# Left-over values and the next chunk's left-over scores placed back to back in an attention loop

## The chip, the core and the metric

The kernel runs on one core of one Trainium2 chip. The metric is the device time of one execution in microseconds (us), measured over several executions; the profile is taken of one of them. In the profiles PE is TensorE (matmuls), PEld its weight loads, DVE the vector engine, ACT the scalar engine, and SP the engine that issues the DMAs (transfers). Ratios are the mean time of one kernel's runs over that of the other kernel's runs of the same rounds, so they are not quite the ratio of the medians quoted here.

Single executions of one kernel scatter by up to 2 us. I therefore use a second measure beside the time: in each trace, the distance from the start of the first column tile of the attention to the start of the last matmul of the kernel. It leaves out the start-up, the launch and the final stores. It is called "first tile to last matmul".

## The reference

It is a Conformer block on 2 x 4000 tokens of width 512: feed-forward, attention, convolution module, feed-forward. What matters here is the attention of one batch:

```python
q, k, v = h @ w_q, h @ w_k, h @ w_v                    # [2, 4000, 512]
scores = jnp.einsum('btd,bsd->bts', q, k) * scale
p = _softmax(scores, axis=-1)
attn = jnp.einsum('bts,bsd->btd', p, v) @ w_o
```

4000 keys are 31 tiles of 128 and 32 left over. That remainder is the subject of the change.

## The kernel before

Queries go in 16 chunks (8 for each batch) of 508 columns; the last chunk of each batch has 444. For each of 31 key tiles there are four score matmuls, an exponential on ACT, an addition to the sums on DVE, and, four tiles later, four value matmuls into four PSUM banks called Y.

```python
for kt in range(KT):                       # KT = 32; tile 31 is the left-over one
    if kt == self.TAIL_AT:                 # 18
        self.tail_scores(g)
    if kt < KT - 1:
        ...                                # 4 score matmuls, Exp, addition to acc
    if kt == KT - 1:
        self.split_sums(g)                 # ...
    def values(kt=kt, p=p, g=g, W=W):
        for dc in range(DC):
            ...                            # for kt == KT - 1: row tiles, K = 32
            self.mm(self.Yb[dc][:, 0:W], self.h[kt][r, dc * 128:(dc + 1) * 128], x[r, 0:W],
                    kt == 0, kt == KT - 1, ..., **at)
        if kt == KT - 1:
            self.finish_queries(g, done)   # copies the Y banks away, schedules projections
    self.lags.append(values)
    ...                                    # popped four tiles later
    hook(g, kt)                            # convolution projections of earlier chunks, loads
```

The left-over scores use a quarter of the array's columns each, so four of them run side by side as column tiles; each takes a quarter of the chunk's queries. The values use a quarter of the array's rows each, four of them side by side as row tiles. They need the same exponentials for all queries on each group of 32 partitions, so the result makes a trip through DRAM:

```python
def tail_scores(self, g):
    ...
    for cc in range(DC):                           # 16 matmuls, 128 rows x 32 columns
        for j, (r, q) in enumerate(parts):
            self.mm(ps[r, 0:n], hT[:, cc, r], self.qT[s][:, cc, q], ..., tile_position=(0, j * REST))
    self.act(self.pq[:, 0:n], ps[:, 0:n], AF.Exp, ...)
    for r, q in parts:
        ...                                        # 4 additions of 32 x 127 on DVE
    self.store(self.pqd[:, 0:n], self.pq[:, 0:n], ...)
    S.dma("SP", k, *[... e.dma_start(self.ptail[r, 0:W]...) for r, q in parts], ...)
```

After a chunk's queries are finished, the chunk goes through the output projection and a layer norm, whose result DMA transposes turn; the convolution projections of that chunk read it in the next chunk:

```python
if kt in (22, 27) and (0 <= g - 1 < tail or g - 1 == tail and (22, 27).index(kt) < self.KEEP):
    pair(g - 1, (22, 27).index(kt))                # two times four matmuls
```

## Time and profile before

| what | before |
|---|---|
| time, median of 4 | 2034.1 us (2033.78 to 2035.38) |
| span of the profiled run | 2030.5 us |
| TensorE busy | 2021.3 us, granted clock 0.999 |
| first tile to last matmul | 1540.93 us |
| visits to tiled mode (column or row tiles) | 32 |
| changes of tile shape | 64 |

The busy time says that TensorE's sequence sets the time, but it doesn't show the time lost between matmuls. What is lost when the tile shape changes is called a drain below. The prediction shows the lines and how the cost of a visit is read from starts.

### The profile page before, as it was taken

The numbers are of one execution on the slowest core, as the hardware profiler recorded it, in microseconds if no ns is written. First come the engines' busy times: TensorE is split into PE (matmuls) and PEld (weight loads), VectorE is DVE, ScalarE is ACT, GpSimd is POOL, SyncE is SP. The second block draws the span as 40 slices with busy tenths as digits, with TensorE's granted clock in tenths as the row PEclk, the third lists the DMA queues.
The fourth block names the chain that finished last, engine by engine and source line by source line (L and its number), as shares of the span: only waits on it lengthen the run. The fifth ranks groups of instructions, "written<-read, shape, count | busy, mean of one in ns | idle before, by whom it ended". The sixth has DMA issues, their size and how long they took to land.

```text
span 2030.5 us, 25096 instructions
## 1 busy us (share of the span) xinstructions
PE 2021.3 (100%) x9874; PEld 1026.5 (51%) x9874; DVE 1089.1 (54%) x2237; ACT 740.0 (36%) x1275; POOL 108.0 (5%) x235
## 2 busy tenths in 40 slices
PE   9999999999999999999999999999999999999998
PEld 5555555554444444445444444444455555555555
DVE  4234443335556667667766676667674543444433
ACT  3433333333333333333333333333345443443433
POOL 1000000000000000000000000000011000000000
PEclk9999999999999999999999999999999999999999
DMA  8122245421101111113521111111143111111111
GB/s 190 48 62 63 53 100 127 96 68 25 20 16 32 27 35 27 32 27 90 122 54 27 29 32 32 27 30 30 44 139 94 32 32 41 32 31 42 30 34 38
DMA packets 264644, 107.03 MB, mean 53 GB/s; under 512 B 204932, under 2 KB 264007, under 8 KB 264519
## 3 DMA queue, kind: packets, MB, share of 16 engines
q1 hardware_dynamic: 263841, 105.01, 21.7%
q8 instruction: 80, 1.31, 0.3%
q14 instruction: 45, 0.37, 0.1%
q10 hardware_dynamic: 678, 0.34, 0.1%
HBM read 35.81 MB, written 23.86 MB: 29 GB/s over the span
## 4 chain that ended last, share of the span: by engine, by line
PE 99%; DVE 0%; ACT 0%; DMA 0%; issue 0%; POOL 0%; DVEq 0%; ACTq 0%
PE s L521 56%; PE y L521 43%; DVE work L633 0%; DMA work<-work 0%; ACT work L571 0%; PE y L549 0%; POOL work L740 0%; PE y L536 0%; DVE work L1376 0%; DVE work L735 0%; DVE work L653 0%; DVE work L568 0%; DVE wff L1254 0%; ACT keys L571 0%; DVE wff L1141 0%
## 5 line engine op out<-in xcount | busy, mean ns | idle before, releaser
L571 ACT ACTIVATE work<-s 128x508 bf16<-128x508 f32 (+3 forms) x1044 | 613.8, 589 | 1197.8 <-PE s L521 1192.4
L521 PE MATMUL s<-work,wff 128*128 128x508 bf16 (+4 forms) x2640 | 628.3, 369 | 1.0 <-DMA work<-work 0.7
L521 PE MATMUL s<-work,keys 128*128 128x508 bf16 (+2 forms) x2240 | 505.8, 356 | 0.0
L521 PE MATMUL y<-wff,work 128*127 128x512 bf16 (+1 forms) x2000 | 501.4, 378 | 0.0
L521 PE MATMUL y<-work,keys 128*128 128x508 bf16 (+1 forms) x1984 | 495.1, 373 | 0.0
L971 DVE TENSOR_TENSOR work<-work 128x508 f32<-128x508 f32 (+1 forms) x480 | 324.3, 676 | 265.2 <-ACT work L571 262.5
L521 PEld LDWEIGHTS s<-work,wff 128*128 128x128 bf16 x2640 | 252.6, 98 | 277.1 <-issue 4.7
L521 PEld LDWEIGHTS y<-wff,work 128*127 128x127 bf16 x2000 | 274.4, 137 | 170.9
L521 PEld LDWEIGHTS s<-work,keys 128*128 128x128 bf16 (+1 forms) x2240 | 195.7, 97 | 228.9 <-ACT work L571 5.8
L521 PEld LDWEIGHTS y<-work,keys 128*128 128x128 bf16 x1984 | 192.1, 97 | 226.7 <-DVE work L568 0.5
L767 DVE SCALAR_TENSOR_TENSOR xt<-y,xt 127x512 bf16<-127x512 f32 x125 | 77.8, 684 | 364.2 <-PE y L521 364.2
L633 DVE BATCH_NORM_STATS2 work<-xt 127x6 f32<-127x512 bf16 x311 | 195.6, 679 | 4.7 <-DMA xt<-in_x_dram 4.6
L521 PE MATMUL s<-work 128*127 128x512 bf16 (+4 forms) x775 | 195.7, 377 | 1.2 <-DVE work L1372 1.2
L640 POOL TENSOR_TENSOR work<-work 127x4 f32<-127x4 f32 (+1 forms) x76 | 76.6, 1008 | 1127.8 <-DVE work L638 1127.8
L521 PEld LDWEIGHTS s<-work 128*127 128x127 bf16 (+2 forms) x775 | 94.3, 124 | 74.7 <-issue 3.0
L653 DVE TENSOR_SCALAR work<-xt,work 127x512 bf16<-127x512 bf16 x309 | 111.7, 408 | 27.6 <-POOL work L640 23.2
L767 DVE SCALAR_TENSOR_TENSOR xt<-s,xt 127x512 bf16<-127x512 f32 x55 | 38.1, 692 | 148.5 <-PE s L521 148.5
L571 ACT ACTIVATE wff<-s 128x508 f32<-128x508 f32 (+2 forms) x83 | 44.0, 531 | 64.2 <-PE s L521 64.1
L767 DVE SCALAR_TENSOR_TENSOR xt<-s,work,xt 127x512 bf16<-127x512 f32 x64 | 48.0, 750 | 31.0 <-PE s L521 30.5
L1152 DVE SCALAR_TENSOR_TENSOR wff<-wff,s 128x508 bf16<-128x508 f32 (+1 forms) x57 | 38.7, 679 | 42.0 <-PE s L521 41.9
L571 ACT ACTIVATE work<-keys,work 128x508 bf16<-128x508 bf16 (+1 forms) x68 | 52.2, 775 | 0.4 <-DVE work L1268 0.2
L1233 POOL COPY wff<-wff 128x1 bf16<-128x1 bf16 x56 | 10.5, 188 | 633.8 <-DVE wff L1152 631.0
(94 smaller groups left out, 439.9 us busy)
## 6 DMA issues: line engine op xcount, KB each, us to landing
keys<-keysd SPq DMA_DIRECT2D x62, 128.0 KB, 2.3
keysd<-work SPq DMA_DIRECT2D x14, 448.0 KB, 3.2
out_dram<-work SPq DMA_DIRECT2D x14, 448.0 KB, 3.2
dcvd<-wff SPq DMA_DIRECT2D x48, 127.0 KB, 1.8
keys<-dcvd SPq DMA_DIRECT2D x12, 508.0 KB, 4.8
xt<-in_x_dram SPq DMA_DIRECT2D x13, 448.0 KB, 4.7
wff<-in_w_ff_a_dram SPq DMA_DIRECT2D x15, 256.0 KB, 4.8
work<-work SPq DMA_TRANSPOSE x208, 2.5
```

The source lines that it names most:

```text
L521: self.S.op("PE", lambda e: e.matmul(out, lhsT, rhs, start=start, stop=stop, **kw), reads=reads, writes=[bank], inc=stop if inc is None el ...
L571: return self.S.op("ACT", lambda e: e.activation(out, in_, func, **kw), reads=reads, writes=writes)
L633: self.S.op("DVE", lambda e: e.bn_stats(self.st[sl][:, ti, 0:6], x), reads=[b_x], writes=[self.b_st[sl][ti]])
L640: S.op("POOL", lambda e: e.tensor_tensor(out=self.rs[sl][:, 0:n], in0=self.mv[sl][:, 0:n, 1], in1=self.neghalf[0:TILE, 0:n], op=ALU.pow), ...
L653: self.S.op("DVE", lambda e: e.tensor_scalar(out, x, self.mv[sl][:, ti, 0:1], self.rs[sl][:, ti:ti + 1], ALU.subtract, ALU.mult), reads=[b ...
L767: self.S.op("DVE", lambda e: e.scalar_tensor_tensor(out=self.XT[g][rows], in0=ps[rows], scalar=scalar, in1=self.XT[g][rows], op0=ALU.mult, ...
L971: S.op("DVE", lambda e, p=p: e.tensor_tensor(out=acc, in0=acc, in1=self.P[p][:, 0:W], op=ALU.add), reads=[self.b_P[p], self.b_acc[s]], wri ...
L1152: self.S.op("DVE", lambda e: e.scalar_tensor_tensor(out=out, in0=th, scalar=1.0, in1=ps[:, 0:W], op0=ALU.add, op1=ALU.mult), reads=[b_ps, ...
L1233: S.op("POOL", lambda e: e.tensor_copy(self.G[gs][:, jj, 0:1], self.G[gp][:, jj, CHUNK:CHUNK + 1]), reads=[self.b_G[gp][jj]], writes=[self ...
```

## The change

Its intent is to visit tiled mode less often: the row tiles of one chunk's left-over values are put directly in front of the column tiles of the next chunk's left-over scores, at key tile 24, so that two visits become one.

```diff
-    TAIL_AT = 18
+    TAIL_AT = (18, 24)
...
-                if kt == self.TAIL_AT:
+                ahead = not self.any_score and g != 0 and g != TCB
+                if kt == self.TAIL_AT[0] and not ahead:
                     self.tail_scores(g)
+                    self.tail_sums(g)
+                if kt == 2 and ahead:
+                    self.tail_sums(g)
+                if kt == self.TAIL_AT[1]:
+                    self.tail_values(g)
+                    if not self.any_score and g + 1 < NCK and g + 1 != TCB:
+                        self.tail_scores(g + 1)
...
-                    if kt == KT - 1:
+                    if kt == KT - 2:
                         self.finish_queries(g, done)
...
+    def tail_values(self, g):
+        W = width(g)
+        for dc in range(DC):
+            r = slice(dc * REST, (dc + 1) * REST)
+            self.mm(self.Yb[dc][:, 0:W], self.h[KT - 1][r, dc * 128:(dc + 1) * 128], self.ptail[r, 0:W],
+                    False, False, ..., tile_position=(dc * REST, 0))
```

The four DVE additions move out of `tail_scores` into `tail_sums`. Chunks 0 and 8 open a batch and keep their scores at their own tile 18.

More of the change, by code (lines that the diff above doesn't have):

```diff
@@ L980, in values @@
                     for dc in range(DC):
-                        r, x, b_x, at = slice(0, 128), self.P[p or 0], self.b_P[p or 0], {}
-                        if kt == KT - 1:
-                            r, x, b_x, at = slice(dc * REST, (dc + 1) * REST), self.ptail, self.b_ptail, {"tile_position": (dc * REST, 0)}
-                        self.mm(self.Yb[dc][:, 0:W], self.h[kt][r, dc * 128:(dc + 1) * 128], x[r, 0:W],
-                                kt == 0, kt == KT - 1, [self.b_h[kt], b_x], self.b_Y[dc],
-                                inc=kt == KT - 1 or dc == DC - 1, **at)
-                    if kt == KT - 1:
+                        self.mm(self.Yb[dc][:, 0:W], self.h[kt][:, dc * 128:(dc + 1) * 128], self.P[p][:, 0:W],
+                                kt == 0, kt == KT - 2, [self.b_h[kt], self.b_P[p]], self.b_Y[dc],
+                                inc=kt == KT - 2 or dc == DC - 1)
+                    if kt == KT - 2:
                         self.finish_queries(g, done)
-                self.lags.append(values)
+                if kt < KT - 1:
+                    self.lags.append(values)
                 if g == 0 and kt < LAG:
@@ L1028, in tail_scores @@
         self.act(self.pq[:, 0:n], ps[:, 0:n], AF.Exp, [b_ps], [self.b_pq], scale=SCALE)
-        for r, q in parts:
-            acc = self.acc[s][r, q]
-            S.op("DVE", lambda e, acc=acc, r=r: e.tensor_tensor(out=acc, in0=acc, in1=self.pq[r, 0:n], op=ALU.add),
-                 reads=[self.b_pq, self.b_acc[s]], writes=[self.b_acc[s]])
         self.store(self.pqd[:, 0:n], self.pq[:, 0:n], [self.b_pq], [self.b_pqd])
@@ L1037, in tail_scores, with tail_sums @@
                          for r, q in parts], reads=[self.b_pqd], writes=[self.b_ptail])
+    def tail_sums(self, g):
+        s, n = g % 2, width(g) // 4
+        for j in range(4):
+            r = slice(j * REST, (j + 1) * REST)
+            acc = self.acc[s][r, j * n:(j + 1) * n]
+            self.S.op("DVE", lambda e, acc=acc, r=r: e.tensor_tensor(out=acc, in0=acc, in1=self.pq[r, 0:n], op=ALU.add),
+                      reads=[self.b_pq, self.b_acc[s]], writes=[self.b_acc[s]])
+    def tail_values(self, g):
+        W = width(g)
+        for dc in range(DC):
+            r = slice(dc * REST, (dc + 1) * REST)
+            self.mm(self.Yb[dc][:, 0:W], self.h[KT - 1][r, dc * 128:(dc + 1) * 128], self.ptail[r, 0:W], False, False,
+                    [self.b_h[KT - 1], self.b_ptail], self.b_Y[dc], inc=dc == DC - 1, tile_position=(dc * REST, 0))
     def key_tile(self, b, kt):
```

## The prediction

> **What bounds the kernel now.** I read the page first, then the groups with shapes kept apart, then the order of TensorE's work around the two special blocks, then the waits of the weight loads.
>
> ```profile
> span 2030.5 us, 25096 instructions
> ...
> PE 2021.3 (100%) x9874; PEld 1026.5 (51%) x9874; DVE 1089.1 (54%) x2237; ACT 740.0 (36%) x1275; POOL 108.0 (5%) x235
> ...
> PEclk9999999999999999999999999999999999999999
> ...
> PE 99%; DVE 0%; ACT 0%; DMA 0%; issue 0%; POOL 0%; DVEq 0%; ACTq 0%
> ```
>
> TensorE is busy all the time at the full clock, and the chain that ended last is TensorE for 99%. So only what shortens TensorE's own sequence can shorten the kernel, and a wait hidden on another engine is worth nothing. Busy time is not enough here, because a TensorE that drains still looks busy. The change touches only the attention stage (about 480 to 1508 us), where each of 16 query chunks has 31 full key tiles and 32 left-over keys. For the left-overs, 16 score matmuls run as column tiles (128 rows by 32 columns) and 4 value matmuls as row tiles (32 rows by 128 columns):
>
> ```profile
> L521 PE MATMUL s<-work,keys 128*32 128x127 bf16 x224 | 5.7, 222 | 0.0
> L521 PE MATMUL y<-wff,keys 32*128 32x508 bf16 x56 | 5.5, 383 | 0.0
> L521 PEld LDWEIGHTS s<-work,keys 128*32 128x32 bf16 x256 | 3.7, 96 | 6.6 <-ACT work L571 5.8 <-issue 0.8
> L521 PEld LDWEIGHTS y<-wff,keys 32*128 32x128 bf16 x64 | 1.6, 90 | 6.6 <-issue 6.6
> ```
>
> The reader should see that the weight-load path is idle for 6.6 us before each kind, so 6.6/16 = 0.41 us in front of each block. Before ordinary loads it is far less (221.1 us over 1936 loads, 0.11 us). What these blocks cost is to be read from starts, not from durations. In the order of TensorE's work (start, length, group):
>
> ```profile
> 480.65 1.03 PE L521 MATMUL s<-work 128*128 128x508 bf16 x4
> 481.51 1.02 PE L521 MATMUL s<-work,keys 128*128 128x508 bf16 x4
> 482.38 1.02 PE L521 MATMUL y<-work,keys 128*128 128x508 bf16 x4
> 483.32 1.38 PE L521 MATMUL s<-work,keys 128*32 128x127 bf16 x20
> 484.54 1.02 PE L521 MATMUL y<-work,keys 128*128 128x508 bf16 x4
> ```
>
> The x20 row is the 16 column tiles and, merged with them, four full score matmuls.
>
> ```profile
> 512.87 1.02 PE L521 MATMUL y<-work,keys 128*128 128x508 bf16 x4
> 513.73 1.02 PE L521 MATMUL s<-work,keys 128*128 128x508 bf16 x4
> 514.68 0.39 PE L521 MATMUL y<-wff,keys 32*128 32x508 bf16 x4
> 515.01 1.04 PE L521 MATMUL s<-work 128*128 128x508 bf16 x4
> 515.88 0.38 PE L521 MATMUL s<-work,keys 128*128 128x508 bf16 x1
> ```
>
> Four full matmuls take 0.86 us from start to start (480.65 to 481.51, 512.87 to 513.73), so one takes 0.215. Column block: 482.38 to 484.54 is 2.16 us, less two ordinary groups (1.72) leaves 0.44. Row block: 513.73 to 515.88 is 2.15, less 1.72 leaves 0.43. Both must stream 508 columns (4 waves of 127; or 4 row tiles at once), worth 0.215. The remaining 0.22 in each is therefore two changes of tile shape of 0.11 us, one in and one out.
>
> The single records show the pieces. Before the first column tile 307 ns pass instead of 214 (93 lost); from the last column tile to the full matmul 154 ns, where its 127 columns need 55 (99 lost). Into the row tiles 310 ns (96 lost), out 315 (101 lost). The first full matmul after either block takes 224 to 226 ns instead of about 216 (some 10 lost). All 16 blocks of each kind repeat this within 4 ns for equal widths, except where neighbours of another width stand beside them. A constant loss is not a data wait; the page's "<-ACT work L571 5.8" is the semaphore that fired last, long before.
>
> **What the Trainium skill says.** "TensorEngine Tiling (Array Packing)", Key Properties: "Changing tiling mode (not just tile) drains the TensorE". The trace agrees: every change costs 93 to 101 ns. It does not say whether row mode to column mode drains as full to tiled does. "TensorE: Matmul & The Clock Gate", Part 3, has packed matmuls start about 4 ns apart; here the four row tiles start 3 to 4 ns apart. "Perfetto Trace Analysis", Tensor Engine Instruction, says that a matmul's recorded end is a model and its start is observed; this is why I use starts only.
>
> **The change part by part.**
> Removed: nothing in arithmetic. The instruction orders show the same 256 column and 64 row matmuls, the same 64 small additions, 16 stores and 64 reloads.
>
> Moved on TensorE: the row block goes from behind the fourth score tile of the next chunk to key tile 24 of its own, and there the next chunk's column block follows at once. Each batch's first chunk (0 and 8) keeps its scores at tile 18, and the last chunks (7 and 15) have nothing to follow. So 14 pairs are adjacent, and 2 column and 2 row blocks stay alone. Visits to tiled mode fall from 32 to 14 + 4 = 18, and changes of shape from 64 to 14 x 3 + 4 x 2 = 50.
>
> Worth of one pair: gone are the way out of the row block (101 + 10 ns) and the way into the column block (93 ns), 204 ns; new is the row-to-column change. I take it as a full drain: the first column load cannot begin until all rows are free, as now the first full load cannot. It should stand about 310 ns after the last row tile, where 212 are streaming: 98 ns. Net 204 - 98 = 106 ns. The estimate is 14 x 0.106 = 1.5 us, all on the path, since TensorE waits for nothing else there.
>
> Moved on DVE: four additions of 32x127, 0.28 us each (1.12 us), go from tile 18 to tile 2 of the chunk. In the stretch of tiles 1 to 3 DVE idles 1.03 us before its additions, so it falls behind by perhaps 0.1 us. Two steps later DVE copies two of the Y banks before TensorE may overwrite them; TensorE waited for that only this much:
>
> ```profile
> PEld y L521 <- issue: 6.6, 16, 0.4
> ...
> PEld y L521 <- DVE work L568: 0.5, 2, 0.4
> ```
>
> The banks now finish with a staggered full group, each 0.215 us behind the last, instead of all at the end of the row tiles, so the first ones can be copied sooner before the 0.86 us or more of scores that follow. I expect this wait to vanish rather than grow: 0 to 0.4 us gained, of which I count 0.1.
>
> Moved in the queue: the trip of the exponentials through DRAM gets nearly a whole chunk, except in chunks 0 and 8, where scores at 18 are read at 24. Chunk 8 is the tight one, since key loads crowd the queue (start, length):
>
> ```profile
> 1019.24 0.58 SPq L588 DMA_DIRECT2D pqd<-wff  x1
> 1021.01 1.75 SPq L1036 DMA_DIRECT2D wff<-pqd  x4
> ...
> 1026.65 1.02 PE L521 MATMUL s<-work,keys 128*128 128x508 bf16 x4
> ```
>
> The scores ran at 1012.74, but the store was issued only at 1019.24; the last of the reloads landed at 1024.11 by the trace. Tile 24 begins at 1026.65, so 2.5 us are spare. "DMA: Bandwidth & Descriptors" puts a transfer's fixed cost at about 2 us; here these land in a median of 1.8.
>
> Sum: -1.5 - 0.1 = -1.6 us; 2034.2 - 1.6 = 2032.6.
>
> **The rivals.**
> 1. The row-to-column change is cheaper, or free. For: neither mode is the full array, and the skill is silent. Against: a column load needs all 128 rows, which the row tiles hold. Then a pair saves up to 204 ns, 14 x 0.204 = 2.9 us: 2031.3.
> 2. The row-to-column change costs as much as going through full mode (about 200 ns). For: both masks change at once. Against: 93 to 101 in all four known changes, whatever the direction. Then nothing is gained: 2034.2.
> 3. A new data wait takes the place: in chunk 8 (2.5 us spare now, once) or at tile 2 on DVE (at most about 0.1 us in each chunk). It would give 2033 to 2035.
> 4. The four row matmuls vanish behind the others (0.43 x 14 = 6 us). Against: they still stream 508 columns on the same array, and column tiles occupy all rows. I give it almost nothing.
>
> **Range and chances.** Rivals 1 and 2 are 2031.3 and 2034.2; the three runs of before lie 1.6 us apart (2033.78 to 2035.38), so the runs alone blur the result by some 0.8 us. I take 2031.2 to 2034.0 as the range for 8 times in 10. Two per cent are 41 us; no rival reaches a sixth of that. Faster 0.01, within 0.985, slower 0.005.
>
> **What would show it.** Right: 18 tiled visits, 14 of them rows then columns; some 310 ns from last row tile to first column tile; 307 to 310 in and 154 out as now; no wait for DVE before the first Y matmul of a chunk; the row tiles of chunk 8 still 307 to 310 ns behind their neighbour. Wrong: about 215 ns there (rival 1) or over 400 (rival 2); a "DMA wff" or "DVE" wait in front of a tiled block (rival 3); TensorE gaps at the chunk's boundary, where the slot of tile 31 now holds no matmuls at all and the next chunk's first scores come 0.86 us sooner after the last ones, which the softmax's engines must follow.

## More of the kernel before

The waits of TensorE between 1480 and 1492 us, in the last chunk (total, times, longest):

```profile
PE s L521 <- DMA work<-work: 0.7, 1, 0.7
```

## The result and the profile after

The changed kernel takes 2033.18 us (median of 4, 2032.89 to 2033.78) against 2034.1 (4 runs): 0.9 us less. The ratio is 0.9995, with a 95% interval of 0.9977 to 1.0012, so by the times alone it is the same. The forecast of 2032.6 with 2031.2 to 2034.0 holds it. From first tile to last matmul it is 1539.83 us, 1.10 less than before. That is less than the 1.6 us of my sum, and the traces are exact enough to ask where the rest went.

The page after:

```profile
span 2029.4 us, 25092 instructions
...
PE 2020.6 (100%) x9872; PEld 1028.0 (51%) x9874; DVE 1091.3 (54%) x2237; ACT 740.1 (36%) x1275; POOL 108.1 (5%) x235
...
PE 99%; DMA 0%; DVE 0%; ACT 0%; SPq 0%; issue 0%; ACTq 0%
```

The bound has not moved. The order of TensorE's work around the first pair (start, length, group; the x20 row again holds 16 column tiles and four full matmuls):

```profile
495.25 1.02 PE L522 MATMUL y<-work,keys 128*128 128x508 bf16 x4
496.20 0.39 PE L522 MATMUL y<-wff,keys 32*128 32x508 bf16 x4
496.52 1.38 PE L522 MATMUL s<-work,keys 128*32 128x127 bf16 x20
497.74 1.02 PE L522 MATMUL y<-work,keys 128*128 128x508 bf16 x4
```

From 495.25 to 497.74 are 2.49 us, less two ordinary groups (1.72) leaves 0.77 for the pair, where the two separate visits cost 0.44 + 0.43. In the single records, 310 ns pass into the row tiles, 312 or 313 from the last row tile to the first column tile, and 153 or 154 out (147 for the short chunks). I had estimated 310 for the new change. An ordinary matmul of 508 columns takes 214 ns, so 98 or 99 are lost (100 or 101 against the 212 ns of streaming that the prediction took here). All 14 pairs look like this. Chunk by chunk the changed kernel gains 0.103 us on the kernel before.

The weight loads of the tiled blocks between 479 and 1508 us (count, busy, mean ns, idle before):

```profile
L522 PEld LDWEIGHTS s<-work,keys 128*32 128x32 bf16 x256 | 3.7, 96 | 4.0 <-issue 4.0
L522 PEld LDWEIGHTS y<-wff,keys 32*128 32x128 bf16 x64 | 1.6, 90 | 6.6 <-issue 6.6
```

The idle time before column loads falls from 6.6 to 4.0 us. The releaser that the page named before, ACT with 5.8 us, is gone. In e7 below, where the column blocks stand alone again with the same 307 or 308 ns in front of them, the same view puts 5.9 of 6.7 us down to "issue" and 0.4 to ACT. So the name of the releaser says nothing of the cause here.

Up to 1482 us the kernel has gained 1.48 us. Then it loses some. The last chunk, in the kernel before:

```profile
1488.79 0.91 PE L521 MATMUL y<-work,keys 128*128 128x444 bf16 x4
1490.40 1.89 PE L521 MATMUL s<-work,wff 128*128 128x508 bf16 x8 [0.69 <-DMA work<-work]
```

The same place in the changed kernel:

```profile
1487.70 0.91 PE L522 MATMUL y<-work,keys 128*128 128x444 bf16 x4
1489.75 1.89 PE L522 MATMUL s<-work,wff 128*128 128x508 bf16 x8 [1.14 <-DMA work<-work]
```

A group of four matmuls of 444 columns takes 0.75 us from start to start. From 1488.79 to 1490.40 are 1.61 us, so 0.86 are lost; from 1487.70 to 1489.75 are 2.05, so 1.30 are lost. The convolution projection of chunk 14 waits for its transposed layer norm. The wait was there before, and it grew by 0.44 us. The "0.69" and "1.14" are counted from the modelled end of the matmul in front; starts give the full loss.

Why it grew: the chain of output projection, layer norm and four DMA transposes begins in the early tiles of chunk 15 and ends at its own pace. TensorE's work between the chain's beginning and the projection at tile 22 used to include chunk 15's column block at tile 18 (0.42 us). The change took that block out. Counted from DVE's last residual addition of chunk 14, with which the layer norm can begin, TensorE is ready for the projection 0.42 us sooner (after 16.12 us, 16.55 before), and the chain took 0.02 us longer in this execution.

The transposes in the queue of DMA issues, before and after (start, length of the whole group of four):

```profile
1482.83 6.09 SPq L579 DMA_TRANSPOSE work<-work  x4
```

```profile
1482.16 6.12 SPq L580 DMA_TRANSPOSE work<-work  x4
```

The changed kernel's group starts only 0.67 us sooner, where TensorE is 1.09 us sooner (1488.79 against 1487.70), and it takes as long. Three of the four issues take 1.22 to 1.27 us, and one takes longer: 2.20 us before, 2.24 after.

### The profile page after: what moved, and what is told of

The parts are those of the page before. It is cut to its first block, busy times and chain, and to the rows that moved or that the text cites. A ratio compares the mean times of both kernels' runs of the same rounds, so it can differ in the third digit from the quotient of the medians.

```text
span 2029.4 us, 25092 instructions
## 1 busy us (share of the span) xinstructions
PE 2020.6 (100%) x9872; PEld 1028.0 (51%) x9874; DVE 1091.3 (54%) x2237; ACT 740.1 (36%) x1275; POOL 108.1 (5%) x235
## 4 chain that ended last, share of the span: by engine, by line
PE 99%; DMA 0%; DVE 0%; ACT 0%; SPq 0%; issue 0%; ACTq 0%
PE s L522 56%; PE y L522 43%; DMA wff<-in_w_ff_a_dram 0%; ACT work L572 0%; DMA work<-work 0%; SPq L584 0%; DVE work L634 0%; PE y L550 0%; DVE work L569 0%; DVE wff L1272 0%; ACT keys L572 0%; DVE wff L1159 0%; ACT xt L572 0%; PE y L537 0%; DVE work L845 0%
## 5 line engine op out<-in xcount | busy, mean ns | idle before, releaser
L572 ACT ACTIVATE wff<-s 128x508 f32<-128x508 f32 (+3 forms) x83 | 43.6, 527 | 72.2 <-PE s L522 72.0
```

Source lines behind the costliest of these rows:

```text
L572: return self.S.op("ACT", lambda e: e.activation(out, in_, func, **kw), reads=reads, writes=writes)
```

## The experiments

The theory (A): 14 pairs are worth 1.5 us, all of it on TensorE's path up to chunk 15, and 0.44 us of this came back as a longer wait there. Rivals: the missing part is scatter or missing records (B); pairs are worth less (C); each pair counts for its 0.106 us wherever it stands (D). All the kernels gave correct results. For each the time is compared with the kernel before on the same chip; "tile" is a key tile of a chunk.

### e1 and e2: the waiting projection moved to tile 26

The edit, on the kernel before (e1) and on the changed kernel (e2):

```diff
-            if kt in (22, 27) and (0 <= g - 1 < tail or g - 1 == tail and (22, 27).index(kt) < self.KEEP):
+            if kt in (22, 27) and 0 <= g - 1 < tail:
                 pair(g - 1, (22, 27).index(kt))
+            if kt == 26 and g - 1 == tail:
+                pair(g - 1, 0)
```

> The kernel before, with the first half of chunk 14's convolution projection in chunk 15 moved from key tile 22 to key tile 26. Theory A (a wait of 0.86 us for the transposed layer norm stands in front of that projection in the kernel before, and I overlooked it): the wait vanishes, about 0.9 us less than before (2033.2), and no gap over 0.1 us is left in TensorE's attention. Theory B (the gap is only missing records of the trace): no change, a gap stays.

> The changed kernel with the same move of that projection from tile 22 to tile 26. Theory A (14 pairs save 1.5 us up to there, but 0.44 us of it came back because the same wait grew from 0.86 to 1.30 us): 1.3 us less than the changed kernel, 2.3 to 2.4 us less than before (2031.8), and 1.5 us less than the kernel before with the same move. Theory B (the missing 0.4 us is scatter between executions): 0 to 0.3 us less than the changed kernel. Theory C (pairs are worth less than 106 ns each): against the kernel before with the same move only 1.0 us less.

Measured: e1 2034.57 us and e2 2033.38 us, against 2034.36 for the kernel before on that chip. First tile to last matmul: e1 1540.75, e2 1539.66. The wait at the projection is gone in both: 188 and 187 ns from the matmul in front, one ordinary step. But I missed on the time: only 0.18 us came of it in each. TensorE now waits at the end of the attention, in e2 (start, length, group):

```profile
1505.29 0.73 PE L522 MATMUL y<-work,keys 128*128 128x444 bf16 x3
1506.72 1.11 PE L522 MATMUL s<-work 128*127 128x1 bf16 x9 [0.70 <-DVE work L1078]
```

These are the sums, which wait for DVE. The depthwise work that hangs on the projection came four tiles later, right in front of the last additions and of the splitting of the sums. Over the first two of the one-column matmuls it costs 0.65 us in e1 and 1.10 in e2. By the numbers alone e2 came out as the rivals had said: 0.18 us less than the changed kernel (B), 1.09 less than e1 (C; A had said 1.5). Only the trace, with the new wait, speaks for A. One half of rival B is out, the missing records, since the wait was real and could be removed; its other half, scatter, is left to e5 and e6. The move itself was a bad one: it exchanged one wait for another. The test had to be made again with a smaller move.

### e3 and e4: chunk 15 keeps its scores

```diff
-                ahead = not self.any_score and g != 0 and g != TCB
+                ahead = not self.any_score and g not in (0, TCB, NCK - 1)
...
-                    if not self.any_score and g + 1 < NCK and g + 1 != TCB:
+                    if not self.any_score and g + 1 < NCK - 1 and g + 1 != TCB:
                         self.tail_scores(g + 1)
```

In e4 also `if kt == (28 if g == NCK - 1 else self.TAIL_AT[1])` in front of `tail_values`.

> The changed kernel, but chunk 15 keeps its left-over scores at its own tile 18, so 13 pairs instead of 14; its left-over values stay at tile 24. Theory A: the wait in front of the projection at tile 22 goes back to 0.86 us, because the column block fills 0.44 us of it, and everything up to there comes 0.34 us sooner (0.773 for the pair less 0.433 for the row block alone); but the trip of the exponentials through DRAM is queued behind the transposes and lands only at about 1492.7 us, so the row block at tile 24 waits some 0.5 us: 0.1 to 0.3 us slower than the changed kernel. Theory D (each pair lost costs its 0.106 us, no more and no less): 0.1 us slower, with no wait in front of the row block.

> As the run before it, but chunk 15's left-over values stand at tile 28 instead of 24, so that their data have landed. Theory A: no wait in front of the row block, 0.3 us FASTER than the changed kernel although it has one pair fewer (about 1.4 us less than before). Theory D: 0.1 us slower than the changed kernel.

Measured: e3 2032.41 us, e4 2033.25 us (before 2034.36). First tile to last matmul: 1539.43 and 1539.76, so 0.40 and 0.08 us less than the changed kernel, with one pair fewer. e4's sign is as theory A said and against D, but the size is not, and e3 came out faster where I had said slower.

The cause is in the transposes. The two kernels are the same up to the projection, yet its wait is 0.63 us in e3 and 1.12 in e4. In every run with this wait I measured the slowest of the four transposes and the distance from chunk 14's last residual to the projection:

| run | slowest transpose issue, us | last residual to projection, us | difference, us |
|---|---|---|---|
| before | 2.20 | 17.40 | 15.20 |
| changed | 2.24 | 17.42 | 15.18 |
| e3 | 1.98 | 17.17 | 15.19 |
| e4 | 2.46 | 17.66 | 15.20 |
| e7 | 1.77 | 16.95 | 15.18 |
| e8 | 2.19 | 17.37 | 15.18 |

So one transpose issue scatters from run to run, and the wait scatters with it; the rest of the chain does not. Why that issue is slow stays open. Put at a transpose of 2.24 us, the wait is 0.89, 0.88 and 0.89 us in before, e3 and e4, where chunk 15's column block stands at its tile 18, and 1.30, 1.30 and 1.29 in the changed kernel, e7 and e8, where it does not. This shows that the wait grew because the block went. With the same 2.24 us, e4 would be 0.30 us faster than it (0.08 + 0.22; expected 0.3), and e3 0.14 faster (0.40 - 0.26). In e3 the row block did wait for the trip through DRAM, but 0.16 us and not 0.5. The start gap into the row tiles there is 440 ns instead of 284, and the profile names the reload for its weight loads in this stretch:

```profile
PEld y L522 <- DMA wff<-pqd: 0.5, 1, 0.5
```

(This counts the whole idle time of the load path, of which about 0.37 us is the usual drain.) D falls: a pair fewer made the kernel faster, in that place.

### e5 and e6: the projection moved to tile 24 only

The edit is that of e1 with 24 instead of 26: e5 on the kernel before, e6 on the changed kernel.

> The kernel before, with chunk 14's last projection moved from tile 22 only to tile 24 of chunk 15. At tile 26 (e1) the wait at the projection went, but the DVE work that hangs on it came so late that TensorE waited 0.5 us for the sums at the end of the attention. Theory A: at tile 24 both waits are absent; from the first column tile to the last matmul 0.85 us less than the kernel before (1540.93), so about 1540.1. Theory B (the stage is bound by DVE's chain there in any case): the end still waits, 0.2 us less or nothing.

> The changed kernel with the same move to tile 24. Theory A: no wait at the projection and none at the sums: from the first column tile to the last matmul 1.3 us less than the changed kernel (1539.83), so about 1538.5, and 1.5 to 1.6 us less than the kernel before with the same move: the 14 pairs at 0.106 us each, all on the path. Theory B: at most 0.3 us less than the changed kernel, and 1.1 us less than the kernel before with the move. In time about 2032.0.

Measured: e5 2033.81 us, e6 2032.55 us (before 2034.78 on that chip; e6's ratio to it is 0.999, interval 0.9976 to 1.0003). First tile to last matmul: e5 1540.07 and e6 1538.54, both as theory A said; in time I had said about 2032.0 for e6. e6 in the last chunk:

```profile
1489.38 0.91 PE L522 MATMUL y<-work,keys 128*128 128x444 bf16 x4
1490.23 0.37 PE L522 MATMUL y<-wff,keys 32*128 32x444 bf16 x4
1490.53 0.92 PE L522 MATMUL s<-work,keys 128*128 128x444 bf16 x4
1491.29 0.91 PE L522 MATMUL y<-work,keys 128*128 128x444 bf16 x4
1492.04 1.24 PE L522 MATMUL s<-work,wff 128*128 128x508 bf16 x5
```

The projection follows 0.75 us after the group in front, with no wait, and there is none at the sums. With the wait out of both kernels the change is worth 1.54 us, near the 1.6 of my sum. With it in both, it is worth 1.10. The difference is 0.44 us: what the wait took. Rival B had said 1.1 for the two with the move, so its scatter is out too. e6 is also faster than both kernels in the traces, by 2.39 us against the kernel before and 1.30 against the changed one; its five times (2032.24 to 2032.62) lie below all nine of the kernel before on that chip (2033.47 to 2035.25).

### e7 and e9: the same moves without the adjacency

```diff
                 if kt == self.TAIL_AT[1]:
                     self.tail_values(g)
-                    if not self.any_score and g + 1 < NCK and g + 1 != TCB:
-                        self.tail_scores(g + 1)
+                if kt == self.TAIL_AT[1] + 2 and not self.any_score and g + 1 < NCK and g + 1 != TCB:
+                    self.tail_scores(g + 1)
```

e7 is this on the changed kernel, e9 on e6.

> The changed kernel with the next chunk's column block at tile 26 instead of directly behind the row block at tile 24: every other move stays, only the adjacency goes. If the adjacency is what saves: 32 visits to tiled mode, 93 to 101 ns lost at each change of shape, 14 x 0.106 = 1.5 us more than the changed kernel, which makes it 0.4 us SLOWER than the kernel before, since the wait at chunk 15's projection stays at 1.3 us. If it is the earlier or later places that save: the same time as the changed kernel.

> The kernel of e6 (changed kernel, projection at tile 24, so no wait left in the last chunk) with the column block two tiles behind the row block as in e7. e7's verdict needed a correction of 0.47 us, because one of four DMA transposes was that much quicker there and shortened the wait; here no wait can hide or add anything. If adjacency is worth one change of tile shape in each of 14 pairs: from first column tile to last matmul 1.48 us more than e6 (1538.54), so 1540.0. If adjacency is worth only what the raw e7 shows: 0.98 us more, 1539.5.

Measured: e7 2034.99 us (before 2034.78), e9 2034.01 us (before 2034.50 on its chip). First tile to last matmul: e7 1540.81, 0.98 more than the changed kernel. Its transpose was 0.47 us quicker, and with that corrected it is 1.45. e9, where nothing waits, settles it without a correction: 1539.99, 1.45 us more than e6. That is 104 ns for each of 14 pairs. e7's row and column blocks (start, length, group):

```profile
495.50 1.02 PE L522 MATMUL y<-work,keys 128*128 128x508 bf16 x4
496.45 0.39 PE L522 MATMUL y<-wff,keys 32*128 32x508 bf16 x4
496.78 1.03 PE L522 MATMUL s<-work,keys 128*128 128x508 bf16 x4
...
499.37 1.02 PE L522 MATMUL y<-work,keys 128*128 128x508 bf16 x4
500.31 1.38 PE L522 MATMUL s<-work,keys 128*32 128x127 bf16 x20
501.53 1.02 PE L522 MATMUL y<-work,keys 128*128 128x508 bf16 x4
```

Each block costs again what it cost before: 495.50 to 496.78 is 1.28 us (0.43 over a group of 0.855), and 499.37 to 501.53 is 2.16 us (0.44 over two groups). So the adjacency saves, and the earlier places hardly do: e9 is only 0.08 us below e5. Rival C (pairs worth less than 106 ns) falls too, but for 2 ns. By the times, e7 is the same as the kernel before (ratio 1.0002). In the traces it is 0.12 us faster, where I had said 0.4 slower; with both transposes put at 2.24 us it is 0.32 slower, since without adjacency the longer wait in chunk 15 is left with little to pay for it.

### e8: columns before rows

`tail_scores` was split, so that the 16 matmuls and the exponential come first, then `tail_values`, then the trip through DRAM (which must not overwrite the values' operand earlier).

```diff
                 if kt == self.TAIL_AT[1]:
+                    nxt = not self.any_score and g + 1 < NCK and g + 1 != TCB
+                    if nxt:
+                        self.tail_scores(g + 1, False)
                     self.tail_values(g)
-                    if not self.any_score and g + 1 < NCK and g + 1 != TCB:
-                        self.tail_scores(g + 1)
+                    if nxt:
+                        self.tail_trip(g + 1)
```

> The changed kernel with the two blocks of a pair in the other order: column tiles of the next chunk's scores, then row tiles of this chunk's values (the exponentials' trip through DRAM starts behind both). If every change of tile shape drains alike: some 153 ns from the last column tile to the first row tile (55 of streaming and 98 of drain), the pair costs the same 0.77 us and the kernel the same time within 0.2 us. If only the row-to-column direction has the cheap or dear switch: a difference of up to 14 x 0.1 = 1.4 us.

Measured: 2033.61 us (before 2034.78); first tile to last matmul 1539.76, 0.07 less than the changed kernel, of which the quicker transpose explains 0.05. The pair in e8:

```profile
495.52 1.02 PE L522 MATMUL y<-work,keys 128*128 128x508 bf16 x4
496.47 0.41 PE L522 MATMUL s<-work,keys 128*32 128x127 bf16 x16
496.81 0.39 PE L522 MATMUL y<-wff,keys 32*128 32x508 bf16 x4
497.14 1.03 PE L522 MATMUL s<-work,keys 128*128 128x508 bf16 x4
```

From the last column tile to the first row tile 153 or 154 ns pass, 55 of them streaming, so 98 or 99 are lost, as in the other direction. The order within a pair does not matter.

### e10: DVE's additions back at tile 18

On e6:

```diff
-                if kt == 2 and ahead:
+                if kt == 18 and ahead:
                     self.tail_sums(g)
```

> The kernel of e6 with DVE's four small additions of the left-over exponentials back at tile 18 instead of tile 2. If their new place at the start of a chunk neither costs nor gains: 1538.5 from first column tile to last matmul, within 0.05 us of e6, and no wait of TensorE for DVE before the first value matmul of a chunk in either. If tile 2 had delayed DVE's copies of the Y banks: up to 0.4 us less than e6.

Measured: 2032.49 us (before 2034.50); first tile to last matmul 1538.54, the same as e6 to 1 ns. The place of these 1.12 us of DVE work per chunk costs and gains nothing.

## Why the prediction was right, and where its sum was not

**The bound: right.** TensorE holds 99% of the chain that ended last, before and after.

**The cost of a change of tile shape: right.** I had 93 to 101 ns for the known changes and assumed about 98 for the unknown one between rows and columns. It is 98 or 99, in both directions (after, e8). The prediction counted the streaming as 214 ns on the way out and as 212 here; that is 2 ns in the pair. Rival 1 (free) and rival 2 (double) fall by this, and so does rival 4, which would have saved 6 us.

**The worth of a pair: right.** 106 ns expected, 104 measured by taking the adjacency away (e9), with 14 pairs.

**"All on the path, since TensorE waits for nothing else there": this step was wrong.** TensorE waited 0.86 us for the transposed layer norm in chunk 15, and the waits of TensorE name it. I had looked for waits in front of the tiled blocks and at the chunk's boundary, not for waits in places that the change does not touch. The end of the layer norm's chain does not move with TensorE's work at tile 18, so what the change removes in front of it is not gained. The wait grew to 1.30 us, and of the 1.48 us that were saved up to there 0.44 were lost: 0.42 since TensorE came earlier, 0.02 since the chain took longer. Rival 3, a new data wait, came near, but the wait was in neither of the two places that it named, and it was not new. The other sign of being wrong, gaps at a chunk's boundary, did not come: with the tiled blocks left out, no TensorE start in the attention stage of the changed kernel but this one stands over 0.32 us behind the one in front.

**The wait for DVE's copies of Y: the direction was right, the size not.** I counted 0.1 us; it was a single gap of 25 ns over an ordinary step, and it is gone.

**Chunk 8's trip through DRAM: right.** I had 2.5 us to spare. In the changed kernel the last reload is issued at 1022.23 and the row block starts at 1026.38; with 1.8 us to landing, the median before, about 2.3 are spare, and the start gap is the ordinary 310 ns.

The account from first tile to last matmul: 14 pairs -1.45, the DVE wait -0.03, the longer wait in chunk 15 +0.44, and -0.06 at the end. Of the last, 0.05 is at the sums by TensorE, whose first one-column matmul stood directly behind the last row block before, 80 ns in front of its follower; now it stands behind full matmuls, and the distance is 28 ns. The sum is -1.10, as measured. My 1.6 was off by this one term, and by little else.

The forecast stayed in its range because the overlooked term is smaller than the range. That is luck in part: the range was made for the cost of the shape change and the scatter of the runs, and not for a wait that grows.

## What to carry to other kernels

In this kernel each change between full, row and column tiles lost 93 to 101 ns, so small tiled blocks are best gathered into one visit, and it is the starts, not the durations, that show the cost. One such place was in neither the prediction nor the count of visits: near 999 us, in both kernels, stand four matmuls of 63 weight columns, for which no tile position is asked. The first starts 307 or 308 ns behind a full matmul, and the next full one 312 ns behind the last, where 214 to 216 ns are ordinary. Before counting a saving on the critical engine as gained, list every wait of that engine downstream, also where the change touches nothing, and ask whether the chain behind that wait starts before or after the place of the saving. Work that waits should be moved no further than it needs: two tiles removed the wait here, and four exchanged it for a wait for another engine.

## What the Trainium skill lacked or had wrong

- "TensorEngine Tiling (Array Packing)", Key Properties, says that a change of tiling mode drains TensorE, but gives no size and does not name row to column as such a change. It is one: 98 or 99 ns were lost in either direction between row and column tiles, and 93 to 101 between full and tiled. Nor does it say that the first full matmul behind a tiled block loses a little more: 224 to 226 ns passed to its follower instead of 214 to 216, where the widths on both sides were equal.
- "TensorE: Matmul & The Clock Gate", Part 2, tells of weight loads pulled ahead of running matmuls. Nothing there says that the pull-ahead stops at a change of shape. Here the first load of a tiled block starts 1 to 5 ns before its own matmul, and an ordinary load some 210 ns before it.
- "DMA: Bandwidth & Descriptors", DMA Transpose (X-bar), does not say how far the time of one transpose issue scatters. Of the four in a row here (one for each row tile of a chunk), three took 1.21 to 1.27 us each and one took 1.66 to 2.54 us from run to run. This scatter passed into the kernel's time wherever TensorE waited for them.
